# A scan and feed-forward kernel on one core: unit 0's scan in four tiles, the first transfers in halves over two queues, and a new order of the first steps

## The chip, the cores and the metric

The kernel runs on one core of one Trainium2 chip. Its engines are TensorE (PE, with its weight loads PEld), VectorE (DVE), ScalarE (ACT), GpSimd (POOL) and SyncE (SP), which here only issues transfers. The metric is the device time of one execution in microseconds. A time is the median of several runs.

## The reference: what is computed

Two blocks follow each other. The first is a chunked scan over a sequence of 768 positions, for 4 sequences (batch) of 8 heads each, with head dimension 32 and state size 16:

```
for each chunk:
    L  = exp(cum[i] - cum[j]) for i >= j, else 0        # products of the decays a
    M  = (C B^T) * L
    y  = M x  +  (C state) * exp(cum)
    state = exp(sum(log a)) * state + sum_j (B_j x_j) * exp(cum[-1] - cum[j])
```

The second is a feed-forward block on the result, 3072 tokens of 256 values: `h = y @ w_in` (256 x 2048), `g = h * cos(h)`, `out = g @ w_out` (2048 x 256). The two weights come in as 64-bit floats, the rest as 32-bit floats.

## The kernel before, in words

**Tiling.** The sequence is cut into six chunks of 128 positions. Chunk 0 is cut once more into two units of 64 positions (unit 0 and unit 1), so that TensorE gets its first large products early. A unit's partitions hold two halves s of 64 rows (sequences 2s and 2s+1), and p (or q in the loads) picks one of the two sequences of a half.

**Steps of a unit.** `spread_a` (L330) spreads the decays over the partitions with small matmuls; `decays0` (L345) turns them into products of decays with a scan on VectorE (`lam`, L353). `turn0` (L363) transposes B and C on TensorE (L370) and ScalarE copies them out of PSUM (`cut` L377, `take` L373). `reach0` (L380) is one matmul (L383) and one scan (L385) for unit 1's decays from its start. `inner` (L394) makes g = C B^T (L401), `weights` (L405) multiplies g by `lam` on VectorE (L410), and `finish0` (L413) makes y: for unit 1 first what the old state adds (L426), then M x (L434) and the new state's sum (L444); ScalarE copies y out (L454 for unit 0, L452 for unit 1) and `take_s0`, `take_s1` copy the new state (L462). `add_s1` adds the decayed old state to unit 1's on GpSimd (L469, L471). PSUM is handed out in turn: `pair` (tag "scan", two buffers of two banks), tags "h" and "o" (two buffers of one bank each). A new tile of a tag waits until the tile two before it has been read.

**Weights.** `fetch` (L195) loads a piece of w_in or w_out, 512 KB each, eight of either. A piece is turned from 64-bit to 32-bit words in two steps: `grade` (L213) is two activations on ScalarE (L227, L225) and one operation on GpSimd (L228); `join` (L235) is two operations on VectorE (L241, L243) and one on GpSimd (L251), which writes the finished piece. For the first piece `grade` and `join` go by halves (n=2).

**Feed-forward steps.** A step n covers 256 tokens' worth of one unit and 256 of the 2048 columns. `first(n)` is the product with w_in (L649), `wind(n)` the range reduction (ScalarE L654, VectorE L656), `gate(n)` the sine (ScalarE L661), `gated(n)` the product h * cos(h) (VectorE L666), `second(n)` the product with w_out (L710). In chunk 0 the steps alternate between unit 0 (even n) and unit 1 (odd n); steps 2j and 2j+1 need piece j of w_in and of w_out. `hp`, the result of `first`, has two buffers, so `first(n)` waits for `gated(n-2)`.

**Order.** The whole order is written out by hand: within an engine, instructions run in the order in which the program issues them. `first_steps` (L892) holds the steps 0 to 3 of the feed-forward block together with the rest of unit 1's scan; from step 4 on a loop (L948) takes over, in which a step does `first`, `wind`, `grade` of the next piece, `gate`, `join` of this step's piece, `gated`, the scans of chunk 1 (`halved`, L877, VectorE L496), and `second(n-2)`. In the opening transfers go through the queue of SP, save the two pairs of loads of C for units 0 and 1, which are issued from ScalarE's queue (L125); a transfer's issue stands in the order of its engine like any other instruction. `clips` (L835) prepares the decays for later chunks and writes them to memory, after which chunk 1's loads start. `fill` (L81) issues matmuls whose result nobody reads.

The two places in the order that the prediction comes back to, the opening and the first steps, are these lines of the kernel before:

```
    spread_a(0, 0, (0, 1), wide[0])
    spread_a(0, 1, (0,), wide[1])
    cut0, take0 = turn0(0, [bank([P, 2, P], "tp", "h") for _ in range(2)])
    spread_a(0, 1, (1,), wide[1])
    spread_a(1, 0)
    for p in range(2):
        decays0(0, p)
```

Of the kernel before, what the change touches and what calls it, by code (L numbers as in the profile page):

```python
# [25 lines left out]
def kernel(  # L26
# [91 lines left out]
    def load_bc(k, which=(0, 1), eng=nc.sync):  # L118

        if k not in bcs:  # L120
            both = loads.tile([P, 2, 2, 2, H, N], FP32, tag="bc", name="bc")
            bcs.update({i: both[:, i] for i in range(2)})
        for w in which:
            for s in range(2):
                eng.dma_start(out=bcs[k][s * W:(s + 1) * W, w].rearrange("p q h n -> p (q h) n"),  # L125
                              in_=(B, C)[w][2 * s:2 * s + 2, :, k * W:(k + 1) * W, :]
                              .rearrange("b h i n -> i (b h) n"))

    def load_x(k):
# [3 lines left out]
        for s in range(2):  # L133
            nc.sync.dma_start(out=xrs[k][s * W:(s + 1) * W].rearrange("p q h d -> p (q h) d"),
                              in_=x[2 * s:2 * s + 2, :, k * W:(k + 1) * W, :]
                              .rearrange("b h i d -> i (b h) d"))
# [98 lines left out]
    def join(which, i, es=(0, 1)):  # L235


        parts = held.get((which, i), ())
        for e in es[:len(parts)]:
            high, bits, last = parts[e]  # L240
# [12 lines left out]
    load_bc(0, (0,))  # L253
    load_bc(0, (1,), nc.scalar)
    fetch("in", 0)
    load_x(0)
    load_bc(1, (0,))
    fetch("in", 1)
    load_x(1)
# [12 lines left out]
    load_bc(1, (1,), nc.scalar)  # L272
# [33 lines left out]
    share_a(1, G, 0, H)  # L306
    G.memset(along1[:, :, 0:1], 0.0)
    G.tensor_scalar(out=a0[:, 1], in0=a0[:, 1], **clip)
    for p in range(2):
# [9 lines left out]
                    axis=mybir.AxisListType.XY, op=ALU.add)  # L319

# [9 lines left out]
    def spread_a(k, p, parts=(0,), tile_=None):  # L330

        n = 2 if tile_ else 1
        if (k, p) not in spread:
            spread[k, p] = [t.rearrange("p (h i) -> p h i", i=W) for t in (
                [tile_[:, i, 0:H * W // 2] for i in range(2)] if tile_ else
                [bank([P, H * W], "a_ps", "o")])]
        for i in parts:
            for s in range(2):
                b = 2 * s + p
                PE.matmul(spread[k, p][i][s * W:(s + 1) * W],  # L340
                          lhsT=those[:, b:b + 1].to_broadcast([P, W]),
# [3 lines left out]
    def decays0(k, p):  # L345

        if p == 0:
            lams[k] = scan.tile([P, 2, H, W], FP32, tag="lam", bufs=4, name="lam")
# [682 lines left out]
```

## Time and profile before

| what | value |
|---|---|
| three runs | 377.05, 378.02, 380.63 us; median 378.02 us |
| the profiled execution | 377.81 us, of which the span of the profile is 376.0 us |
| granted TensorE clock | 0.998 of full speed |
| busy share: PE, PEld | 97 %, 87 % |
| busy share: DVE, POOL, ACT | 75 %, 57 %, 46 % |
| moved by transfers | 31.54 MB in 124425 packets, 93568 of them under 512 B |

The profile is of one execution. Its times are microseconds from the start of the span. A group is a line of the program on one engine with its operation and its tile; behind a group or an instruction stands the idle time of its engine just before it and what ended that idle time. The chain of waits follows the work that ended last back from the end. A window is a stretch of the span with the busy time of each engine in it. Matmuls overlap each other in TensorE, so a busy PE is not one at its peak.

### The profile page before, as it was taken

Reading aid. Unit: us, or ns where it says so; the run is one execution under the profiler, and the core shown is the slowest. Engines: PE = TensorE matmul, PEld = TensorE weight load, DVE = VectorE, ACT = ScalarE, POOL = GpSimd, SP = SyncE. Lnnn points to the kernel's source line nnn. Section 1 sums busy time; section 2 is a strip of 40 time slices with the busy share of each in tenths; the row PEclk is TensorE's granted clock in tenths of the full one; section 3 lists DMA queues with packets and bytes.
Section 4 is the critical chain, followed back from the end, with each engine's and each line's share of the span. In section 5 each row is a group of like instructions: output and inputs, shape, how many; then the busy total and the mean of one; then the engine's idle time right before and its main releaser. Section 6 shows DMA issues by size and latency. Waiting matters only on the chain.

```text
span 376.0 us, 8691 instructions
## 1 busy us (share of the span) xinstructions
PE 365.3 (97%) x3274; PEld 326.0 (87%) x3274; DVE 281.7 (75%) x471; ACT 172.7 (46%) x295; POOL 215.1 (57%) x336
## 2 busy tenths in 40 slices
PE   8978999999999999999999999999999999999995
PEld 4667887888899899999899998999999989999994
DVE  5958999989889957987767987766887872553553
ACT  3586576444354335344434445434444443444442
POOL 5568664489947545674454693363775344544451
PEclk9999999999999999999999999999999999999999
DMA  9999987415536641745223654211020000010011
GB/s 123 227 272 249 254 210 143 98 14 132 127 84 81 125 109 16 125 114 136 28 42 33 124 140 94 51 16 16 3 40 8 13 17 2 2 28 2 5 26 28
DMA packets 124425, 31.54 MB, mean 84 GB/s; under 512 B 93568, under 2 KB 120288, under 8 KB 124384
## 3 DMA queue, kind: packets, MB, share of 16 engines
q1 hardware_dynamic: 120064, 30.60, 38.3%
q10 hardware_dynamic: 4320, 0.39, 0.9%
q8 instruction: 26, 0.43, 0.5%
q14 instruction: 15, 0.12, 0.1%
HBM read 27.64 MB, written 3.34 MB: 82 GB/s over the span
## 4 chain that ended last, share of the span: by engine, by line
PE 71%; POOL 7%; DVE 7%; SPq 5%; DMA 5%; issue 3%; ACT 1%; POOLq 0%; DVEq 0%; ACTq 0%
PE hp L649 34%; PE o L748 30%; SPq L151 3%; POOL words L685 2%; PE y L588 2%; DMA xr<-in_x_dram 2%; PE g L546 2%; DVE mag L243 1%; DVE mag L241 1%; DMA words<-in_moe_w_out_dram 1%; PE y L581 1%; DVE w L656 1%; POOL gd L691 1%; DVE gT L666 1%; SPq L110 1%
## 5 line engine op out<-in xcount | busy, mean ns | idle before, releaser
L649 PE MATMUL hp<-yT,w_in 128*128 128x256 f32 x768 | 183.4, 382 | 3.8 <-POOL la L838 1.9
L649 PEld LDWEIGHTS hp<-yT,w_in 128*128 128x128 f32 x768 | 139.4, 190 | 23.5 <-issue 5.9
L691 POOL TENSOR_TENSOR gd<-gT 128x256 f32<-128x256 f32 x79 | 59.0, 747 | 99.5 <-DVE gT L666 93.0
L661 ACT ACTIVATE w<-w,quarter 128x512 f32<-128x512 f32 x96 | 69.2, 721 | 78.8 <-DVE w L656 78.8
L656 DVE SCALAR_TENSOR_TENSOR w<-hp,k 128x512 f32<-128x512 f32 x96 | 65.4, 681 | 39.5 <-ACT k L654 39.1
L654 ACT ACTIVATE k<-hp 128x512 int32<-128x512 f32 x96 | 57.1, 595 | 81.2 <-PE hp L649 80.9
L666 DVE TENSOR_TENSOR gT<-hp,w 128x512 f32<-128x512 f32 x96 | 65.2, 680 | 34.5 <-ACT w L661 25.7
L748 PE MATMUL o<-words,gd 128*128 128x128 f32 x474 | 65.9, 275 | 0.0
L748 PEld LDWEIGHTS o<-words,gd 128*128 128x128 f32 x474 | 59.3, 192 | 0.0
L496 DVE TENSOR_TENSOR_SCAN lam<-arow,unit 128x512 f32<-128x512 f32 x40 | 56.8, 1421 | 0.0
L748 PEld LDWEIGHTS o<-w_out,gT 128*128 128x128 f32 x316 | 47.5, 191 | 4.0
L748 PE MATMUL o<-w_out,gT 128*128 128x128 f32 x316 | 48.0, 274 | 0.0
L694 POOL TENSOR_TENSOR gd<-gT,gd 128x128 f32<-128x128 f32 x79 | 44.4, 562 | 6.2
L693 POOL TENSOR_TENSOR gd<-gT,gd 128x128 f32<-128x128 f32 x79 | 44.0, 556 | 6.2
L710 PE MATMUL o<-w_out,gT 128*128 128x256 f32 x128 | 30.2, 380 | 1.2 <-POOL w_out L251 1.2
L567 DVE TENSOR_TENSOR m<-g,lam 128x256 f32<-128x256 f32 x80 | 30.9, 415 | 0.5
L748 PE MATMUL o<-words,gT 128*128 128x128 f32 x158 | 30.6, 275 | 0.0
L748 PE MATMUL o<-w_out,gd 128*128 128x128 f32 x158 | 30.5, 275 | 0.0
L710 PEld LDWEIGHTS o<-w_out,gT 128*128 128x128 f32 x128 | 24.2, 190 | 4.8 <-POOL w_out L251 1.6
L748 PEld LDWEIGHTS o<-words,gT 128*128 128x128 f32 x158 | 24.0, 192 | 0.0
L748 PEld LDWEIGHTS o<-w_out,gd 128*128 128x128 f32 x158 | 24.0, 192 | 0.0
L765 DVE TENSOR_TENSOR sum<-ps,sum 128x256 f32<-128x256 f32 (+1 forms) x27 | 16.7, 645 | 0.6
(104 smaller groups left out, 268.2 us busy)
## 6 DMA issues: line engine op xcount, KB each, us to landing
arow<-a_cut SPq DMA_DIRECT2D x20, 512.0 KB
words<-in_moe_w_in_dram SPq DMA_DIRECT2D x8, 512.0 KB
words<-in_moe_w_out_dram SPq DMA_DIRECT2D x8, 512.0 KB
out_dram<-sum SPq DMA_DIRECT2D x18, 128.0 KB
blocks<-in_B_dram SPq DMA_DIRECT2D x128, 8.0 KB
blocks<-in_C_dram SPq DMA_DIRECT2D x128, 8.0 KB
xr<-in_x_dram SPq DMA_DIRECT2D x14, 128.0 KB
along<-a_all SPq DMA_DIRECT2D x20, 64.0 KB
```

Of the source, the lines that this page charges most:

```text
L496: V.tensor_tensor_scan(out=lam[c, b][:, hs].rearrange("p h i -> p (h i)"), data0=rows_.rearrange("p h i -> p (h i)"), data1=unit[:, b % 2 ...
L567: V.tensor_tensor(out=m_[js, :, :, is_], in0=g_[js, :, :, is_], in1=l_[js, :, :, is_], op=ALU.mult)
L649: PE.matmul(to_[:, e], lhsT=w_in[:, k, fs], rhs=y[:, k], start=(k == 0), stop=(k == KT - 1), skip_group_check=True)
L654: ACT.activation(k, hp[n], AF.Copy, bias=0.25, scale=INV_2PI)
L656: V.scalar_tensor_tensor(out=w, in0=hp[n], scalar=INV_2PI, in1=k, op0=ALU.mult, op1=ALU.subtract)
L661: ACT.activation(cos, cos, AF.Sin, bias=quarter, scale=TWO_PI)
L666: V.tensor_tensor(out=gT[n], in0=hp.pop(n), in1=cos, op=ALU.mult)
L691: G.tensor_tensor(out=d[:, 0:2], in0=g[:, 1:2].to_broadcast([P, 2, P]), in1=g[:, 3::-3], op=ALU.subtract)
L693: G.tensor_tensor(out=d[:, 2], in0=g[:, 0], in1=d[:, 0], op=ALU.subtract)
L694: G.tensor_tensor(out=d[:, 3], in0=g[:, 2], in1=d[:, 2], op=ALU.subtract)
L710: PE.matmul(o[c, u][:, t], lhsT=g[:, 2 * e + t], rhs=w_out[:, 2 * j + e], start=(j == e == t == 0), stop=(j == NJ - 1 and e == 1), skip_gr ...
L748: PE.matmul(at[q], lhsT=a_[q], rhs=w[q], start=(j == 0 and q in starts), stop=(j == NJ - 1), skip_group_check=True)
```

## The change

**Transfers of chunk 0.** `load_bc` and `load_x` now issue one half (s) at a time and take the queue to issue on. x of unit 0 and of unit 1, and B and C of unit 1, are split: one half goes through SP's queue, the other through ScalarE's. Two of ScalarE's four issues behind the first pair stand where C of unit 1 was issued before; the other two stand later, one behind `take0(0)` (half of B of unit 1) and one behind `grade("in", 0)` (half of x of unit 1).

**Unit 0's scan.** The four quarters of its decays go to four PSUM tiles, where before two tiles held two quarters each; the scans are issued as the quarters come. The decays of unit 1 are shared out on VectorE (`share_a(1, V, 0, H)`), where GpSimd did it before.

**Order of the opening.** The scan of `reach0` comes ahead of unit 0's g; `spread_a(1, 0)` comes behind unit 0's g, and `spread_a(1, 1)` behind unit 1's transposes, which are issued as part of the opening now. The first weight piece is graded and joined whole.

**Order of the first steps.** Unit 1's g (`inner`, now one call for each half t) is issued between the two halves of `first(0)`. The `fill` ahead of unit 1's `weights` goes. `grade("in", 1)` and `units_of_decay` come ahead of unit 1's `weights`. The grading of a piece is moved by one place against the joins; `second(0)` and `second(1)` stand ahead of and behind `first(3)`, where both came behind it; `take_s1` comes one step later, and `add_s1` moves from step 2 to step 6 in the loop.

```diff
-    def load_bc(k, which=(0, 1), eng=nc.sync):
+    def load_bc(k, w, s, eng=nc.sync):
...
             bcs.update({i: both[:, i] for i in range(2)})
-        for w in which:
-            for s in range(2):
-                eng.dma_start(out=bcs[k][s * W:(s + 1) * W, w].rearrange("p q h n -> p (q h) n"),
-                              in_=(B, C)[w][2 * s:2 * s + 2, :, k * W:(k + 1) * W, :]
-                              .rearrange("b h i n -> i (b h) n"))
-    def load_x(k):
+        eng.dma_start(out=bcs[k][s * W:(s + 1) * W, w].rearrange("p q h n -> p (q h) n"),
+                      in_=(B, C)[w][2 * s:2 * s + 2, :, k * W:(k + 1) * W, :]
+                      .rearrange("b h i n -> i (b h) n"))
+    def load_x(k, s, eng=nc.sync):
         if k not in xrs:
...
             xrs.update({i: both[:, i] for i in range(2)})
-        for s in range(2):
-            nc.sync.dma_start(out=xrs[k][s * W:(s + 1) * W].rearrange("p q h d -> p (q h) d"),
-                              in_=x[2 * s:2 * s + 2, :, k * W:(k + 1) * W, :]
-                              .rearrange("b h i d -> i (b h) d"))
+        eng.dma_start(out=xrs[k][s * W:(s + 1) * W].rearrange("p q h d -> p (q h) d"),
+                      in_=x[2 * s:2 * s + 2, :, k * W:(k + 1) * W, :]
+                      .rearrange("b h i d -> i (b h) d"))
...
-    def join(which, i, es=(0, 1)):
-        parts = held.get((which, i), ())
-        for e in es[:len(parts)]:
-            high, bits, last = parts[e]
+    def join(which, i):
+        parts = held.pop((which, i), ())
+        for e, (high, bits, last) in enumerate(parts):
             V.tensor_scalar(out=bits, in0=bits, scalar1=3, scalar2=0x3FFFFFFF,
...
-    load_bc(0, (0,))
-    load_bc(0, (1,), nc.scalar)
+    for s in range(2):
+        load_bc(0, 0, s)
+        load_bc(0, 1, s, nc.scalar)
     fetch("in", 0)
-    load_x(0)
-    load_bc(1, (0,))
+    load_x(0, 0)
+    load_bc(1, 1, 1)
+    load_bc(1, 0, 0)
     fetch("in", 1)
-    load_x(1)
+    load_x(1, 0)
     fetch("out", 0)
...
     ACT.activation(const.tile([P, 1], FP32, name="sine"), quarter, AF.Sin)
-    load_bc(1, (1,), nc.scalar)
+    load_x(0, 1, nc.scalar)
+    load_bc(1, 1, 0, nc.scalar)
     V.memset(a0z[:, :, 0:1], 0.0)
...
     share_a(0, V, 0, 6)
-    share_a(1, G, 0, H)
     G.memset(along1[:, :, 0:1], 0.0)
...
                     axis=mybir.AxisListType.XY, op=ALU.add)
+    share_a(1, V, 0, H)
...
-    def spread_a(k, p, parts=(0,), tile_=None):
-        n = 2 if tile_ else 1
-        if (k, p) not in spread:
-            spread[k, p] = [t.rearrange("p (h i) -> p h i", i=W) for t in (
-                [tile_[:, i, 0:H * W // 2] for i in range(2)] if tile_ else
-                [bank([P, H * W], "a_ps", "o")])]
-        for i in parts:
-            for s in range(2):
-                b = 2 * s + p
-                PE.matmul(spread[k, p][i][s * W:(s + 1) * W],
-                          lhsT=those[:, b:b + 1].to_broadcast([P, W]),
-                          rhs=a0s[k][:, i * H // n:(i + 1) * H // n], start=True, stop=True,
-                          tile_position=(0, s * W), skip_group_check=True)
-    def decays0(k, p):
-        if p == 0:
+    def spread_a(k, p, i=0, n=1, tag="o"):
+        ps = (pair("a_ps")[:, 0] if tag is None else bank([P, 4 * P], "a_ps", tag))
+        ps = spread[k, p, i] = ps[:, 0:H * W // n].rearrange("p (h i) -> p h i", i=W)
+        for s in range(2):
+            b = 2 * s + p
+            PE.matmul(ps[s * W:(s + 1) * W], lhsT=those[:, b:b + 1].to_broadcast([P, W]),
+                      rhs=a0s[k][:, i * H // n:(i + 1) * H // n], start=True, stop=True,
+                      tile_position=(0, s * W), skip_group_check=True)
+    def decays0(k, p, i=0, n=1):
+        if p == i == 0:
             lams[k] = scan.tile([P, 2, H, W], FP32, tag="lam", bufs=4, name="lam")
         flat = "p h i -> p (h i)"
-        parts = spread.pop((k, p))
-        for i, ps in enumerate(parts):
-            hs = slice(i * H // len(parts), (i + 1) * H // len(parts))
-            V.tensor_tensor_scan(out=lams[k][:, p, hs].rearrange(flat), data0=ps.rearrange(flat),
-                                 data1=unit0[:, hs].rearrange(flat), initial=0.0,
-                                 op0=ALU.mult, op1=ALU.add)
+        hs = slice(i * H // n, (i + 1) * H // n)
+        V.tensor_tensor_scan(out=lams[k][:, p, hs].rearrange(flat),
+                             data0=spread.pop((k, p, i)).rearrange(flat),
+                             data1=unit0[:, hs].rearrange(flat), initial=0.0,
+                             op0=ALU.mult, op1=ALU.add)
...
-    def inner(k):
-        gs[k] = g = [pair("g") for _ in range(2)]
+    def inner(k, t):
+        gs[k, t] = g = pair("g")
         bT, cT = turns0[k][:, 0], cuts[k]
-        for p, s, q in ((p, s, 2 * t + q) for t in range(2) for p in range(2) for s in range(2)
-                        for q in range(2)):
-            ss, r = slice(s * W, (s + 1) * W), slice(32 * q, 32 * q + 32)
-            PE.matmul(g[q // 2][ss, q % 2, p * P:(p + 1) * P].rearrange("p (t i) -> p t i", t=2),
+        for p, s, q in ((p, s, q) for p in range(2) for s in range(2) for q in range(2)):
+            ss, q_ = slice(s * W, (s + 1) * W), 2 * t + q
+            r = slice(32 * q_, 32 * q_ + 32)
+            PE.matmul(g[ss, q, p * P:(p + 1) * P].rearrange("p (t i) -> p t i", t=2),
                       lhsT=bT[r, p, ss], rhs=cT[r, p, :, ss], start=True, stop=True,
-                      tile_position=(32 * q, s * W), skip_group_check=True)
+                      tile_position=(32 * q_, s * W), skip_group_check=True)
...
                 for ap in (units[k], lams[k]))
-        V.tensor_tensor(out=m, in0=gs[k][q][:, :, 0:2 * P].rearrange("p k (s i) -> p k s i", s=2),
+        V.tensor_tensor(out=m, in0=gs[k, q][:, :, 0:2 * P].rearrange("p k (s i) -> p k s i", s=2),
                         in1=l, op=ALU.mult)
...
-    def first(n):
+    def first(n, between=None):
         c, f = divmod(n, NF)
...
                           start=(k == 0), stop=(k == KT - 1), skip_group_check=True)
+            if between and e == 0:
+                between()
...
     fill(bank([P, 2, P], "warm", "o"), 1)
-    wide = [pair("a_ps") for _ in range(2)]
-    spread_a(0, 0, (0, 1), wide[0])
-    spread_a(0, 1, (0,), wide[1])
-    cut0, take0 = turn0(0, [bank([P, 2, P], "tp", "h") for _ in range(2)])
-    spread_a(0, 1, (1,), wide[1])
-    spread_a(1, 0)
-    for p in range(2):
-        decays0(0, p)
+    spread_a(0, 0, 0, 2, None)
+    spread_a(0, 0, 1, 2, None)
+    spread_a(0, 1, 0, 2, "h")
+    for p, i in ((0, 0), (0, 1), (1, 0)):
+        decays0(0, p, i, 2)
+    cut0, take0 = turn0(0, [bank([P, 2, P], "tp", "o") for _ in range(2)])
+    spread_a(0, 1, 1, 2, "h")
+    decays0(0, 1, 1, 2)
     cut0()
     take0(0)
+    load_bc(1, 0, 1, nc.scalar)
     scan_reach = reach0(1)
+    scan_reach()
     weigh0(0)
-    grade("in", 0, n=2)
-    inner(0)
-    spread_a(1, 1)
-    scan_reach()
+    grade("in", 0)
+    load_x(1, 1, nc.scalar)
+    for t in range(2):
+        inner(0, t)
+    spread_a(1, 0)
     for q in range(2):
...
     take_s0, _ = finish0(0)
+    cut1, take1 = turn0(1, [pair("tp")[:, 0].rearrange("p (k i) -> p k i", k=4)])
+    spread_a(1, 1)
     for p in range(2):
...
+    def both(k):
+        for t in range(2):
+            inner(k, t)
     def first_steps():
...
-        cut1, take1 = turn0(1, [pair("tp")[:, 0].rearrange("p (k i) -> p k i", k=4)])
         cut1()
...
         take1(1)
-        first(0)
-        inner(1)
+        first(0, lambda: both(1))
         weigh_c(1)
         weigh0(1)
-        fill(bank([P, 4, P], "warm", "o"), 1)
+        rest = grade("in", 1, later=True)
+        rest()
+        units_of_decay()
         for q in range(2):
             weights(1, q)
-        rest = grade("in", 1, later=True)
         wind(0)
-        rest()
-        units_of_decay()
+        rest = grade("out", 0, later=True)
         take_s1, add_s1 = finish0(1)
...
         gate(0)
-        rest = grade("out", 0, later=True)
+        rest()
+        clips()
         gated(0)
-        rest()
         wind(1)
-        take_s1()
-        clips()
+        join("out", 0)
         first(2)
...
         gate(1)
-        join("out", 0)
+        take_s1()
         rest()
         gated(1)
+        second(0)
         wind(2)
+        join("in", 2)
         first(3)
...
         gate(2)
-        join("in", 2)
         rest()
         gated(2)
-        add_s1()
+        second(1)
         wind(3)
-        second(0)
+        join("out", 1)
         rest = grade("in", 3, later=True)
         gate(3)
-        join("out", 1)
         rest()
         gated(3)
-        second(1)
         rest = grade("out", 2, later=True)
...
         rest()
-    first_steps()
+        return add_s1
+    add_s1 = first_steps()
     rest_of_loads()
...
             gated(n)
+            if n == AHEAD + 2:
+                add_s1()
             for do in (*behind, *unsummed):
...
             unsummed.clear()
```

## Prediction

> **What bounds the kernel now.** I read the page's slices first (TensorE is busy nearly throughout, the clock full), then stretches of the span, to see where TensorE still waits:
>
> ```profile
> core 0: us, PE busy (x) PEld busy (x) DVE busy (x) ACT busy (x) POOL busy (x), PEclk, DMA share, GB/s
> ...
> 13.33:21.56 8.23, 7.77 (x178) 5.65 (x179) 5.40 (x8) 5.81 (x14) 4.79 (x8) 1.00 1.10 298
> 21.56:35.25 13.69, 10.63 (x50) 9.04 (x49) 10.41 (x16) 10.09 (x18) 10.63 (x15) 1.00 0.90 262
> 35.25:60.70 25.45, 25.08 (x117) 21.31 (x115) 25.02 (x33) 16.61 (x29) 16.32 (x17) 1.00 0.87 212
> ```
>
> From 35.25, where first(5) starts, TensorE is idle for 0.37 of 25.45 us; its sums there are fixed work that the change leaves alone. What can be won is the time at which that work starts. But in the same row VectorE is busy for 25.02 of 25.45: an earlier TensorE is worth only what VectorE is earlier too. In 13.33 to 35.25 TensorE stands still for 0.46 (y copied out), 1.88, 1.18, and 1.13 of "busy" is the fill. So some 4.6 us are the most that order can win there.
>
> Then the chain of waits, for the opening:
>
> ```profile
> 4.22 7.11 DMA xr<-in_x_dram
> ...
> 11.38 0.72 PE y L434 x45
> 12.11 0.47 PE y L444 x23
> 12.60 0.59 ACT yT L454
> ...
> 13.33 1.97 PE hp L649 x8
> ```
>
> The second half of unit 0's x lands at 11.34, and y, its copy and first(0) follow. The timeline shows what is just behind it:
>
> ```profile
> 5.93 1.27 DVE L353 TENSOR_TENSOR_SCAN lam<-a_ps,unit 128x256 f32<-128x256 f32 x2 [2.41 <-PE a_ps L340]
> 7.70 1.27 DVE L353 TENSOR_TENSOR_SCAN lam<-a_ps,unit 128x256 f32<-128x256 f32 x2 [0.50 <-PE a_ps L340]
> 9.87 1.26 DVE L410 TENSOR_TENSOR m<-g,lam 128x512 f32<-128x512 f32 x2
> 12.47 0.42 PEld L370 LDWEIGHTS tp<-ident,bc 128*128 128x128 f32 x4
> 15.20 0.68 POOL L391 TENSOR_TENSOR rT<-turned,m 128x256 f32<-128x256 f32 x1 [1.45 <-DVE lam L353]
> 15.95 1.29 DVE L410 TENSOR_TENSOR m<-g,lam 128x512 f32<-128x512 f32 x2 [0.82 <-PE g L401]
> 23.44 3.61 PE L649 MATMUL hp<-yT,w_in 128*128 128x256 f32 x16 [1.88 <-POOL la L838]
> 24.42 1.26 POOL L251 TENSOR_TENSOR w_out<-mag,last 128x512 uint32<-128x512 uint32 x1
> 32.17 1.48 DVE L241 TENSOR_SCALAR mag<-mag 128x512 uint32<-128x512 uint32 x1 [1.08 <-POOL mag L228]
> 33.41 1.99 PE L710 MATMUL o<-w_out,gT 128*128 128x256 f32 x8 [1.18 <-POOL w_out L251]
> 35.18 1.12 DVE L241 TENSOR_SCALAR mag<-mag 128x512 uint32<-128x512 uint32 x1
> ```
>
> Unit 0's `weights` end at 11.13, only 0.21 before x. Unit 1's transposes at 12.47 wait for the last half of its B: the trace has it landed at 12.56. The 1.88 ahead of first(2) is put down to `clips` on POOL, which it does not need; first(2)'s weight load had run at 21.25 and w_in's piece was done at 20.32. The trace has packets of 16384 bytes on the queue "q8 instruction" at 14.12, 20.89 (1.07 long) and 25.93, and TensorE stops at its 705th recorded instruction: I read this as TensorE waiting for its program.
>
> **Scan in four tiles.** Now the first scan waits for all four products into its tile (5.93). With a tile per quarter it starts 0.13 behind its own: those end at 5.04, so 5.17. By 7.70 three scans are done, one 0.69 scan is left instead of two (1.27): 0.6 earlier. The product of `reach0` no longer stands behind spread_a(1, 0) (1.03 of TensorE), so it runs at 7.5, g at 8.1 to 8.9, the reach scan (0.70) at 8.33, and `weights` (1.26) at 8.98 to 10.24: 0.9 earlier. The moved share_a(1) (384 wide took 0.56 on VectorE, so 512 wide some 0.75) fits the 2.41 idle ahead of 5.93; without that cover it would cost 0.75.
>
> **Small transfers.** Half of x takes the queue position of half of C, so x lands by 9.8 (the first half's 9.69 plus 0.1) instead of 11.34. What is late next is `weights`: y takes 1.17 from 11.38 to 12.55, so now 10.24 to 11.45, copied by 12.05. But the transfers up to unit 1's B are the same bytes, and with both queues in use the small ones land one after the other now (4.21, 4.96, 5.66, 6.53, 7.60, by turns from ACT and SP). So B is complete at 12.56 as before, the transposes end at 13.13 as before, and TensorE runs in order: spread_a(1, 1), moved behind them, takes 1.08 to 14.15. first(0) starts at 14.0, not 13.33: a loss of 0.7. SP's queue issues one small transfer less ahead of w_in's piece 1 and two less ahead of w_out's piece 0 (0.6 to 0.8 each); the pieces still land one behind the other, 1.1 to 1.8 apart, until 26.5, so this is worth nothing. The Trainium skill's page "DMA: Bandwidth & Descriptors" (Rules for kernel authors) speaks against this part: transfers to two partition halves serialize, and more issuing queues save only issue time. By that rule the halves are worth nothing; by the rows x still gains 1.5 from its place in the order, and the sum is the same, since B holds it.
>
> **First piece whole.** Now its halves are done at 12.60 and 13.75. After: ACT from 8.71 (0.7), POOL 0.61, then on VectorE behind `weights` 0.42 and 0.69, POOL 1.27: 12.7. Ahead of 14.0, so it costs nothing; if ACT starts later than 10.0 it costs.
>
> **Unit 1's g and y.** g waits for take_s0 (14.86) and take1(1) (15.12) on ACT, which hang on the transposes and stay. Now it runs behind first(0), 15.22 to 16.02; then at 14.9 and 15.3 to 15.65, between its halves. `lam` of unit 1 is late next: scan behind spread_a(1, 1), 14.2 to 15.4 (now ended 15.13). `weights` then 15.45 to 16.75 instead of 15.95 to 17.24: 0.5 earlier. The fill goes for nothing, since y waits for `weights`. y ends 1.87 later, 18.6 (19.11). first(0)'s second half ends at 16.4 and its range reduction at 17.7, ahead of the join of w_in's piece 1, so that is as now (20.3). first(1) starts at 19.05, ends at 20.9.
>
> **Program refill.** A packet holds some 250 instructions (0.43 MB for 6548 matmuls and weight loads), and the 705th is again the start of first(2). I take its refill to be asked for one packet earlier, in unit 1's y; that comes 0.5 earlier, so first(2) starts at 22.9. Bounds: 20.9 (refilled in time) and 23.44. The page "Runtime: NRT & Kernel Launch" (Instruction fetch mechanics) calls refills of 256 instructions mostly hidden; by that first(2) would start at 20.9. No term of the sum hangs on it, because of what comes next.
>
> **Order of the steps.** first(1) at 20.9 leads through ACT (0.60) and VectorE (0.69) to `join("out", 0)`: 22.35 to 23.5, POOL 1.27 to 24.8 (now 25.68; its mag no longer stands ahead). second(0) 24.85, first(3) 26.6, second(1) 28.3, first(4) 30.1 (1.73 each), second(2) 31.8. But POOL's next mag (0.61) now stands behind each L251 (1.27), so a join is 3.1 behind the one before it: `join("out", 1)` is done at 32.3, so second(2) at 32.3 and first(5) at 34.05: TensorE leads by 1.2. `clips` runs from 20.3 on POOL instead of 21.75, so its two writes and chunk 1's loads behind them on SP's queue (which waited 4.1 for it) go out 1.4 earlier, behind the pieces: nothing. `take_s1` feeds only add_s1, so its later place is free.
>
> **add_s1** (2.2 on POOL at 29.36) goes from there to step 6. VectorE's 1.08 wait at 32.17 stays (mag at 32.9), so w of step 4 is only 0.3 earlier (34.58 now). L241 and L243 behind it took 1.12 and 0.98 beside POOL, 0.41 and 0.69 alone; POOL has less beside them, so I take half, 0.5: VectorE leads by 0.8 from step 5, and by 0.3 at least. At step 6 add_s1 falls beside a busy VectorE: at worst one L241 goes from 0.41 to 0.84; I take 0.2. POOL itself has room there (16.32 of 25.45 busy). **Sum**: 0.8 - 0.2 = 0.6 us. Against the profiled execution (377.81: the span and 1.8 around it) that is 377.2; the median of the runs is 0.2 above it.
>
> **Rivals.** *All of TensorE's lead comes through*: 1.2, and VectorE's waits that stop first(9), first(12) and chunk 1's y (0.21, 0.23, 0.34) go too: 375.8. For it: VectorE's long rows are contention that may move. Against: 25.02 of 25.45.
> *Nothing comes through*: VectorE leads by 0.3, add_s1 takes 0.4: 377.9.
> *Slower: ScalarE stands at an issue.* ScalarE's fourth issue sat from 3.1 to 4.22, until the first transfer of its queue had landed (4.21), so an issue can wait for a transfer. Behind the new issue after take0 stand L227 and L225 of the first piece, behind the second one the copy of y (L454) and unit 1's transposes. Bounds: no wait (ACT is idle for 0.96 there, an issue takes 0.63 to 0.82), or a wait for w_in's piece 1 (14.27), which puts B of unit 1 some 4.8 later. The nearest row is the last transfer of ScalarE's own queue, 10.45: issue 0.7, landing 3.3 behind it, so B at 14.45 instead of 12.56: 1.9 against the gain of 0.6, 379.1. It decides when B lands later than 13.2.
> *The halves don't do what they say* is in the sum: worth nothing already.
>
> **How the numbers follow.** Chances: forecast 0.42 (376.7 to 377.7 by its own bounds), all of it 0.20, nothing 0.18, slower 0.20. The range reaches from the first rival less 0.4 to the slower one plus 0.3: 375.4 to 379.4. A change under 1% can hardly be told from none here, since the three runs lie 0.9% apart. Faster by over 1% (below 374.2) would need most of the 4.6: 0.07. Slower by over 1% (above 381.8) needs the far end of the last rival: 0.09. Within: 0.84.
>
> **What would show it.** Four scans of L353 from 5.2, `weights` done near 10.2, no wait of y for x; transposes still near 12.5, first(0) near 14.0; y of unit 1 ending near 18.6; the gap ahead of first(2) still there; second(0) at 24.9; first(5) near 34.1; VectorE busy as now in 35 to 60. Wrong if the transposes move, if an issue on ScalarE waits past 9.3, or if VectorE's lead at step 5 is not 0.3 to 1.2.

## The result, and the profile after

The changed kernel takes 391.48 us (median of 4 runs, 390.11 to 391.81), the kernel before 378.75 us beside it (377.05 to 380.63): a ratio of 1.0328, interval 1.0269 to 1.0387. I had forecast 377.2 us in a range of 375.4 to 379.4. The profiled execution took 390.11 us with a span of 388.3 us, 12.3 more than before.

The stretches of the span that the prediction started from, in the changed kernel (columns: stretch, its length, then busy time and number of instructions of each engine, granted clock, share of the DMA engines, GB/s):

```profile
core 0: us, PE busy (x) PEld busy (x) DVE busy (x) ACT busy (x) POOL busy (x), PEclk, DMA share, GB/s
13.33:21.56 8.23, 1.43 (x4) 0.58 (x6) 1.29 (x2) 0.64 (x2) 1.26 (x1) 0.58 1.12 304
21.56:35.25 13.69, 11.03 (x189) 7.39 (x186) 8.01 (x12) 9.32 (x21) 7.20 (x12) 0.87 0.39 91
35.25:60.70 25.45, 24.51 (x104) 20.33 (x103) 19.70 (x28) 14.84 (x26) 16.11 (x17) 0.94 0.91 242
```

The first row says it: TensorE is busy for 1.43 of 8.23 us, where it had 7.77 before, and its clock falls to 0.58. Yet the DMA engines are as busy as before (1.12). VectorE, which the prediction made the limit of the last row (25.02 of 25.45), has room there now: 19.70.

The chain of waits in the opening and the first steps (start, length, what):

```profile
0.75 3.28 DMA bc<-in_C_dram
4.05 6.19 DMA bc<-in_C_dram
10.26 9.83 DMA bc<-in_B_dram
20.82 1.91 PE a_ps L335 x4
22.73 2.01 PE hp L642 x4
29.07 2.01 PE hp L642 x8
34.96 3.68 PE o L705 x8
```

Before, the second half of unit 0's x and then y stood here. Now it is one transfer of 64 KB: half of unit 1's B, issued at 10.26 on ScalarE, which had waited for its own half of C (landed at 10.24). It takes 9.83 us. Behind it stand products at nearly twice their length: 1.98 for a spread that takes 1.08 at full clock, 3.68 for a `second` that takes 1.99.

The timeline around them (start, length, engine, line, operation, tiles; in brackets the idle time before and what ended it). Unit 0's scan is L345, weights L403, transposes L363, spread L335, `first` L642, `second` L705, `clips` L836, `join` L237:

```profile
4.89 1.85 DVE L345 TENSOR_TENSOR_SCAN lam<-a_ps,unit 128x256 f32<-128x256 f32 x3 [0.80 <-PE a_ps L335]
7.43 0.69 DVE L345 TENSOR_TENSOR_SCAN lam<-a_ps,unit 128x256 f32<-128x256 f32 x1 [0.68 <-PE a_ps L335]
8.74 1.26 DVE L403 TENSOR_TENSOR m<-g,lam 128x512 f32<-128x512 f32 x2
10.26 0.62 ACTq L123 DMA_DIRECT2D bc<-in_B_dram  x1
20.13 0.69 PE L363 MATMUL tp<-ident,bc 128*128 128x128 f32 x2 [8.55 <-DMA bc<-in_B_dram]
20.75 1.98 PE L335 MATMUL a_ps<-m,those 128*64 128x512 f32 x4
22.65 2.08 PE L642 MATMUL hp<-yT,w_in 128*128 128x256 f32 x4
25.46 1.29 DVE L403 TENSOR_TENSOR m<-g,lam 128x512 f32<-128x512 f32 x2 [1.46 <-PE g L394]
29.07 3.72 PE L642 MATMUL hp<-yT,w_in 128*128 128x256 f32 x16 [0.46 <-ACT yT L445]
30.66 0.40 POOL L836 TENSOR_SCALAR cut<-a_in 96x256 f32<-96x256 f32 x1
34.96 3.68 PE L705 MATMUL o<-w_out,gT 128*128 128x256 f32 x8 [2.17 <-POOL w_out L247]
```

Up to unit 0's y all went as forecast: scans from 4.89, weights done at 10.00, both halves of unit 0's x landed (7.76 and 9.59) before they are wanted, y without a wait. Then TensorE stands still for 8.55 us. The granted clock is full until 14.60, half until 24.84, full until 35.08, half until 38.49, and full from there to the last few us. From step 12 on every step is 12.4 to 12.5 us behind the kernel before, to the end.

The start of some steps in the profiled executions, for all kernels of this document (us):

| kernel | first(0) | first(1) | first(3) | first(7) | first(12) |
|---|---|---|---|---|---|
| before | 13.33 | 19.57 | 25.17 | 42.15 | 60.76 |
| changed | 22.66 | 29.07 | 38.46 | 53.90 | 73.22 |
| e1: half of B back on SP | 13.78 | 23.72 | 32.93 | 48.36 | 67.67 |
| e2: before, half of B late | 16.26 | 23.96 | 29.14 | 45.53 | 64.14 |
| e3: half of B early on ScalarE | 13.99 | 27.17 | 36.68 | 52.11 | 71.43 |
| e4: halves of B and x on SP | 13.74 | 19.62 | 27.33 | 42.77 | 62.08 |
| e5: x on SP, half of B late | 19.22 | 26.04 | 34.99 | 50.88 | 70.18 |
| e6: as e1, x in long rows | 14.55 | 19.96 | 27.67 | 43.11 | 62.43 |
| e7: as e4, old order of steps | 13.87 | 19.27 | 26.58 | 43.58 | 62.17 |
| e8: as e4, add_s1 back | 13.64 | 19.05 | 28.29 | 43.88 | 62.49 |
| e9: changed, wait filled | 21.58 | 28.85 | 36.57 | 52.00 | 71.33 |
| e10: as e4, two steps exchanged | 14.00 | 19.41 | 27.13 | 41.94 | 61.25 |
| e11: as e10, add_s1 at step 12 | 13.87 | 20.13 | 27.85 | 42.65 | 61.24 |

### The profile page after: what moved, and what is told of

It is laid out like the page before. It is cut to its first block, busy times and chain, and to the rows that moved or that the text cites. A ratio compares the mean times of both kernels' runs of the same rounds, so it can differ in the third digit from the quotient of the medians.

```text
span 388.3 us, 8681 instructions
## 1 busy us (share of the span) xinstructions
PE 368.6 (95%) x3272; PEld 326.7 (84%) x3272; DVE 281.3 (72%) x470; ACT 172.4 (44%) x293; POOL 214.6 (55%) x333
## 4 chain that ended last, share of the span: by engine, by line
PE 76%; DVE 8%; DMA 6%; POOL 5%; issue 2%; SPq 1%; ACT 1%; POOLq 0%; ACTq 0%
PE hp L642 37%; PE o L743 29%; DMA bc<-in_B_dram 3%; PE y L581 3%; DMA bc<-in_C_dram 2%; PE o L705 2%; DVE mag L239 2%; PE g L539 2%; DVE mag L237 2%; POOL words L680 2%; DVE lam L489 2%; DVE w L651 1%; PE y L574 1%; DVE gT L661 1%; POOL gd L686 1%
## 5 line engine op out<-in xcount | busy, mean ns | idle before, releaser
L642 PE MATMUL hp<-yT,w_in 128*128 128x256 f32 x768 | 184.8, 384 | 2.6 <-DVE gT L661 1.9
L642 PEld LDWEIGHTS hp<-yT,w_in 128*128 128x128 f32 x768 | 139.9, 191 | 24.7 <-issue 7.0
L661 DVE TENSOR_TENSOR gT<-hp,w 128x512 f32<-128x512 f32 x96 | 65.2, 679 | 33.7 <-ACT w L656 24.8
L743 PEld LDWEIGHTS o<-w_out,gT 128*128 128x128 f32 x316 | 47.6, 191 | 3.9
L705 PE MATMUL o<-w_out,gT 128*128 128x256 f32 x128 | 32.1, 396 | 2.7 <-POOL w_out L247 2.7
L705 PEld LDWEIGHTS o<-w_out,gT 128*128 128x128 f32 x128 | 25.1, 198 | 7.0 <-POOL w_out L247 3.5
L247 POOL TENSOR_TENSOR w_out<-mag,last 128x512 uint32<-128x512 uint32 x8 | 10.2, 1272 | 14.5 <-DVE mag L239 14.5
```

The source lines that it names most:

```text
L642: PE.matmul(to_[:, e], lhsT=w_in[:, k, fs], rhs=y[:, k], start=(k == 0), stop=(k == KT - 1), skip_group_check=True)
L661: V.tensor_tensor(out=gT[n], in0=hp.pop(n), in1=cos, op=ALU.mult)
L705: PE.matmul(o[c, u][:, t], lhsT=g[:, 2 * e + t], rhs=w_out[:, 2 * j + e], start=(j == e == t == 0), stop=(j == NJ - 1 and e == 1), skip_gr ...
L743: PE.matmul(at[q], lhsT=a_[q], rhs=w[q], start=(j == 0 and q in starts), stop=(j == NJ - 1), skip_group_check=True)
```

## The experiments

The first theory after the result was that this one transfer costs all of it. The rival was that the new order of the steps costs it.

### e1: the half of B on SP again

```diff
     load_bc(1, 0, 0)
+    load_bc(1, 0, 1)
     fetch("in", 1)
...
     take0(0)
-    load_bc(1, 0, 1, nc.scalar)
```

> The changed kernel, with one line moved: the second half of unit 1's B is issued from SP, right behind the first half and ahead of w_in's piece 1, and no longer from ScalarE behind unit 0's take. Theory (this one transfer's place costs the 12.4 us): that B is whole by 12.6 to 13.2, as before (in the changed kernel 20.09); the transposes end near 13.5, first(0) starts at 13.6 to 14.2 (22.66), no half clock in the opening, and the time is 376.5 to 379, a ratio of 0.995 to 1.003 against the kernel before. Rival (the new order of the steps and add_s1's later place cost it): B lands early all the same, but first(7) is still some 9 us or more behind the kernel before, and the ratio stays above 1.02.

Measured: 384.81 us (6 runs) against 378.09 (23 runs of the kernel before, shared by e1 to e4), ratio 1.0183 (1.0150 to 1.0216). B is whole at 12.29 and first(0) starts at 13.78, as the theory had it; the time is not. What TensorE waits for between 5 and 47 us (in total, times, longest):

```profile
PE y L428 <- DMA xr<-in_x_dram: 3.9, 1, 3.9
PE o L706 <- POOL w_out L247: 2.7, 2, 2.2
```

The second half of unit 1's x, which the change also moved to ScalarE, was issued at 11.01 and landed at 21.66 (14 of the 16 shares into which a transfer is split by 17.87, the last two at 21.46 and 21.66). The theory was half right: a transfer's place, but there are two such transfers, and the second one stands ready behind the first.

### e3: the half of B on ScalarE, but early

```diff
     load_bc(1, 1, 0, nc.scalar)
+    load_bc(1, 0, 1, nc.scalar)
...
     take0(0)
-    load_bc(1, 0, 1, nc.scalar)
```

> The changed kernel, with the same transfer still on ScalarE's queue, but issued with its other early ones, ahead of unit 0's take. If the place in time behind the pieces that SP has queued is what makes it slow, it is issued by 7, lands by 13, and the time is 376.5 to 379.5 (ScalarE may stand at the issue, ahead of the take: up to 1.5 us). If ScalarE's queue is what makes it slow, it lands 8 us or more behind its issue again, and the time is above 385.

Measured: 388.40 us (4 runs), ratio 1.0266 (1.0231 to 1.0301): the landing is that of the first case, the time that of the second, for another reason. The half of B is issued at 4.82 and landed at 11.87, so ScalarE's queue is not slow in itself. But again x is late, issued at 11.89 and landed at 25.11:

```profile
PE y L428 <- DMA xr<-in_x_dram: 7.1, 1, 7.1
PE o L706 <- POOL w_out L247: 1.6, 2, 1.1
```

### e4: the half of x on SP too

```diff
     load_x(1, 0)
+    load_x(1, 1)
     fetch("out", 0)
...
-    load_x(1, 1, nc.scalar)
```

This comes on top of e1.

> As the run with the half of B on SP, and the second half of unit 1's x is issued from SP too, behind its first half, so that ScalarE issues nothing behind unit 0's take. If ScalarE's hold at its own issues costs only through that half of B, the time is that of the other run within 0.5 us. If the hold at the issue of x still costs (the first piece's shares and the copies of y stand behind it), this one is 0.5 to 2 us faster.

Measured: 378.85 us (12 runs), ratio 1.0021 (1.0000 to 1.0042). That is 6.0 us less than e1, where at most 2 were expected: what e1 still waited for was the landing of x, and not ScalarE's hold at its issue. With both transfers on SP the loss is gone but for some 0.8 us. x of unit 1 lands at 17.29, first(1) starts at 19.62 (before: 19.57). So the two late transfers make the whole of the +3.3 % but 0.2.

### e2 and e5: the half of B late alone

e2 is the kernel before with only the half of B moved to ScalarE, behind unit 0's take. e5 is the changed kernel with x on SP, so that the half of B is late alone there too. The edit of e2 (`load_bc` also takes the halves that it issues):

```diff
     load_x(0)
-    load_bc(1, (0,))
+    load_bc(1, (0,), ss=(0,))
...
     take0(0)
+    load_bc(1, (0,), nc.scalar, (1,))
```

> The kernel before, with only this moved: the second half of unit 1's B is issued from ScalarE behind unit 0's take instead of from SP. Theory: ScalarE's sequencer stands at it until about 10.3, it lands near 20, TensorE stands still from about 12 and gets half a clock behind it, and the time is some 12 us (10 to 14) above the kernel before, 388 to 392. Rival (the new order of the steps is what costs): less than 4 us.

Measured: 380.77 us (10 runs), ratio 1.0060 (1.0038 to 1.0082). The expected 12 us did not come. Same place behind the take, issued at 10.15, but landed at 15.72: 5.6 us behind its issue in place of 9.8, and TensorE waits 2.44.

What differed was what SP had queued. In e2 both halves of x of unit 1 are in SP's queue beside it: rows of 128 bytes. In the changed kernel SP had pieces of the weights there too: rows of 2048 bytes. That gave the second theory, by packets, and e5 to try it:

```diff
     load_x(1, 0)
+    load_x(1, 1)
...
-    load_x(1, 1, nc.scalar)
```

> The changed kernel, with the second half of unit 1's x issued from SP behind its first half; the half of B stays on ScalarE behind unit 0's take. The runs so far have the half of B late alone (kernel before: 2.0 us by its span of 379.4 against 376.0, landing 15.72) and the half of x late alone (landing 21.66, ratio 1.018). Theory (the DMA engines take the packets of the two queues by turns, one for one, so that a small transfer's 64 rows per engine wait for 64 packets of the other queue: short beside rows of x, some 6.4 us beside pieces of 2048 bytes): the half of B now meets x's 128-byte rows on SP's queue and lands at 15 to 17, and the time is 379 to 384. If a late half of B costs by itself what the changed kernel showed (landing 20.09), it is 387 or more.

Measured: 387.18 us (4 runs, against 378.23, 29 runs shared by e5 to e8), ratio 1.0229 (1.0200 to 1.0257). The landing lies where the second theory put it: issued at 9.70, 15 of its 16 shares landed by 15.31, the last at 16.59 (changed kernel: 16.52 and 20.09). Whether the theory's reason put it there is taken up behind e6. The time does not follow: 379 to 384 was expected and it is 387. Only 4.9 us of it are the wait:

```profile
PE tp L364 <- DMA bc<-in_B_dram: 4.9, 1, 4.9
PE o L706 <- POOL w_out L247: 2.7, 2, 2.2
```

The granted clock is half from 15.42 to 22.24 and from 32.48 to 35.90. The spread that the change put behind these transposes takes 1.97 and the first half of first(0) 2.08 us, 1.8 more than at full clock, and the first `second` 3.27 in place of 1.99. e2 has half clock too (15.93 to 19.34), at first(0), but waits 2.4 us less. So in the changed order a late B costs its wait and then some 3 us more (first(12) is 8.1 behind e4's); in e2 first(12) is 3.4 behind the kernel before, 0.9 more than the wait.

### e6: the same bytes in long rows

The packets of the two queues in the changed kernel, from 16.6 to 23.1, while the half of x moves (queue, number of packets, MB, share of the 16 DMA engines). q10 has packets only while a transfer that ScalarE issued is under way; q1 carries SP's:

```profile
q1 hardware_dynamic: 1080, 2.06, 96.2%
q10 hardware_dynamic: 1058, 0.13, 15.2%
```

The two queues move the same number of packets, 1080 and 1058, though one moves 2.06 MB and the other 0.13. In e5, while the half of B moves (12.8 to 14.8), q1's are rows of x, and both go fast:

```profile
q1 hardware_dynamic: 1266, 0.24, 108.0%
q10 hardware_dynamic: 926, 0.06, 34.5%
```

So the engines seem to take a packet of each queue by turns. A small transfer of 1024 rows then has 64 packets per engine. Beside pieces of the weights, each of them waits for one packet of q1, which takes 93 ns (0.962 x 16 x 6.5 / 1080), and takes 15 itself (0.152 x 16 x 6.5 / 1058): 64 x 0.108 = 6.9 us. That is an estimate from the very stretch that it explains, so it tests nothing by itself. e6 puts it to the test: the late half of x, at the same place on the same queue and of the same 128 KB, but in 64 rows (they are other elements of x, so unit 1's y is not the reference's).

```diff
-    load_x(1, 1, nc.scalar)
+    nc.scalar.dma_start(out=xrs[1][W:2 * W].rearrange("p q h d -> p (q h d)"),
+                        in_=x[2].rearrange("h (p e) d -> h p (e d)", e=H * 2)
+                        .rearrange("h p n -> (h p) n")[0:W])
```

This is on top of e1.

> As the run with the half of B back on SP, so that only the second half of unit 1's x is late on ScalarE's queue (there it landed at 21.66, 10.65 behind its issue, time 384.8). Here the same 128 KB are read at the same place in 64 rows of 2048 bytes in place of 1024 rows of 128: other elements of x, so y of unit 1 is computed from wrong data. Theory (packets by turns, one for one): four packets per engine in place of 64, so it lands within 1.5 us of the time at which the queue reaches it, by 17.5, and the time falls to that with x on SP, 378 to 380. Rival (ScalarE's queue comes after SP's whatever the packets, or the bytes share the bandwidth): it lands at 20 or later and the time stays at 383 to 386.

Measured: 380.02 us (10 runs), ratio 1.0055 (1.0031 to 1.0079). Issued at 11.71, 15 of 16 shares landed by 16.32, the last at 17.72; TensorE's wait of 3.9 for unit 1's x is gone. Of the 6.0 us between e1 (384.81) and e4 (378.85), 4.8 are back by the size of the rows alone. From 13.5 to 16.5 ScalarE's queue moves its 0.13 MB in 78 packets, where 0.13 MB were 1058 above:

```profile
q1 hardware_dynamic: 1051, 0.65, 79.7%
q10 hardware_dynamic: 78, 0.13, 22.9%
```

The Trainium skill's page "DMA: Bandwidth & Descriptors" (Queues, rings and completion order) says that each engine goes round the queues it has work for by packets; the equal counts above and e6 agree with it, and it is the rule to which the prediction had paid no heed.

For the half of B it explains less than the theory had it. These are the changed kernel's packets from 10.9, where the issue of that half ended, to 14.5 (the first line), and from 14.5 to 15.5:

```profile
q1 hardware_dynamic: 1463, 0.98, 101.7%
q1 hardware_dynamic: 225, 0.15, 70.8%
q10 hardware_dynamic: 975, 0.06, 68.7%
```

Up to 14.5 q10 has no packet: what SP had issued before this transfer (the rest of w_in's piece 1, half of x, nearly all of w_out's piece 0) moved first. Then nearly the whole half of B moved within 1 us. Only its last share, at 20.09, met the later pieces of the weights. In e5 it was issued ahead of w_out's piece 0 (9.70 against 10.68), and its first row moved at 12.41. So its place in the order of issue over both queues goes with its late start, and turns by packets with its last share only; no run tells the two apart for B, and why it started so late was not tried. In e1, too, it is only the last two shares of x that moved beside the weights (q10 has 102 packets from 17.5 to 21.5).

### e7 and e8: what the rest of the change is worth

e7 is e4 with the steps behind first(0) in the order of the kernel before, add_s1 too, without the fill: the new opening alone. e8 is e4 with add_s1 alone put back.

```diff
         second(1)
+        add_s1()
         wind(3)
...
-            if n == AHEAD + 2:
-                add_s1()
```

> The new opening alone, with both late halves on SP: scan in four tiles, x of unit 0 in halves over two queues, g of unit 1 between the halves of first(0), no fill; behind first(0) the steps are in the order of the kernel before, with add_s1 in its old place. Theory (in the run with the new order VectorE reached step 5 0.63 us late, 35.21 against 34.58 for its second w, since join of w_in's piece 3 stood behind POOL's): here that w is at 34.3 to 34.7, first(11) within 0.4 of the kernel before, and the time 376.5 to 378.5, ratio 0.996 to 1.001. Rival (the opening itself costs): not faster than the run with the new order, 378.9.

> The new opening with both late halves on SP and the new order of steps, but add_s1 back ahead of wind(3) in the opening's steps. Theory (add_s1's later place cost 0.5 to 0.7: in the run with it first(11) and first(12) went from 0.59 to 1.31 behind the kernel before): first(12) is 0.5 to 0.9 behind in place of 1.31, and the time is 378 to 378.6. Rival (2.2 us more of POOL ahead of join of w_in's piece 3 is worse, since VectorE already waits 1.44 for POOL there): first(7) 1.2 to 2.5 behind in place of 0.62, time 379.3 to 381.

Measured: e7 378.29 us (12 runs), ratio 0.9997 (0.9979 to 1.0016); e8 379.09 (12 runs), 1.0015 (0.9993 to 1.0036). The new opening is worth nothing by itself, as its first steps show: first(0) 0.54 later, first(1) 0.30 earlier. What was expected of e7 behind them did not come: in its profiled execution (379.27) TensorE stood still for 3.49 within first(2), the range reduction that started at 34.58 in the kernel before starts at 36.00, and first(11) is 1.4 behind the kernel before. e8 can't be read: its profiled execution had half clock from 25.21 to 28.62, where e4 had none, so that it fits the rival's number (first(7) 1.73 behind) for another reason. The intervals of e4, e7 and e8 overlap.

### e9: TensorE kept busy during the wait

```diff
+    fill(bank([P, 4, P], "warm", "o"), 7)
     cut1, take1 = turn0(1, [pair("tp")[:, 0].rearrange("p (k i) -> p k i", k=4)])
```

This is the changed kernel, with both late halves.

> The changed kernel with both late halves, and seven fills of TensorE (1.1 us each, products that nothing reads) behind unit 0's y, where TensorE waits 8.55 us for the half of B. Nothing else moves. Theory (part of the 12.4 us is the granted clock, 0.5 from 14.60 to 24.84 behind that wait: spread 1.98 in place of 1.08, first half of first(0) 2.08 in place of 1.13): the transposes still start at 20.1, first(0) at 21.6 to 21.9 in place of 22.66, first(1) at 27.0 to 27.6 in place of 29.07 or, if x of unit 1 holds it there, at 28.0; with 1.85 more if the second half-clock stretch (35.08 to 38.49) goes too. Time 386.5 to 390.5. Rival (the lower clock costs nothing that x's late landing doesn't cost anyway): first(1) within 0.3 of 29.07 and the time at 391.

Measured: 392.49 us (4 runs, 388.27 to 393.37; against 378.35, 23 runs shared by e9 to e11), ratio 1.0338 (1.0286 to 1.0390): above the expected 386.5 to 390.5, and not faster than the changed kernel (1.0328). Its profiled execution is the one of 388.27. There the clock is full throughout the steps, and the two parts come out as follows. first(0) starts 1.08 earlier (21.58), but first(1) only 0.22 (28.85), since the half of x then holds y: the rival's answer. The second stretch of half clock is gone, and first(3) is 1.89 earlier (36.57), which stays to the end. The wait for w_out's piece is still there:

```profile
PE o L705 <- POOL w_out L247: 2.7, 2, 2.2
PE tp L363 <- DMA bc<-in_B_dram: 2.5, 1, 2.5
PE y L427 <- DMA xr<-in_x_dram: 0.5, 1, 0.5
```

The other three executions took 391.82 to 393.37 at a mean clock of 0.986 to 0.990 (profiled: 0.998), so they had half clock somewhere in spite of the fills. What the clock costs is thus shown for one execution only, and that a fill buys it back is not shown.

### e10 and e11: the rest of the loss

In e4 VectorE is late at step 5, as this stretch of its timeline shows. The join of w_in's piece 3 waits for its mag on GpSimd, and the second range reduction behind it (`wind`, L653) starts at 35.21; in the kernel before it started at 34.58:

```profile
33.74 0.82 DVE L237 TENSOR_SCALAR mag<-mag 128x512 uint32<-128x512 uint32 x1 [1.44 <-POOL mag L225]
34.60 0.69 DVE L239 SCALAR_TENSOR_TENSOR mag<-words,mag 128x512 uint32<-128x512 uint32 x1
35.21 0.68 DVE L653 SCALAR_TENSOR_TENSOR w<-hp,k 128x512 f32<-128x512 f32 x1
```

e10 exchanges two steps of e4, and e11 moves add_s1 to step 12 as well:

```diff
+        rest = grade("in", 3, later=True)
         join("out", 1)
-        rest = grade("in", 3, later=True)
...
-            if n == AHEAD + 2:
+            if n == NF - 4:
                 add_s1()
```

> The new opening and order with both late halves on SP, and two steps exchanged: w_in's piece 3 is graded ahead of the join of w_out's piece 1, so that its mag on POOL runs before that join's POOL operation and not behind it. Theory (VectorE reached step 5 0.63 later than in the kernel before because this mag came 1.44 late): the wait of 1.44 ahead of that join goes, the second w behind it starts at 33.7 to 34.2 in place of 35.21, first(7) is 0 to 0.8 ahead of the kernel before in place of 0.62 behind, and the time is 377 to 378. Rival (TensorE's own gaps hold it): within 0.3 of 378.9.

> As the run with the two steps exchanged, and add_s1 at step 12 instead of step 6. Theory (at step 6 its 2.6 us of POOL lie beside VectorE's joins and lengthen them: first(11) and first(12) lost 0.46 and 0.24 there): these 0.7 go, and the time is 0.3 to 0.7 below the other run. Rival (at step 12 VectorE is just as full, or the state comes too late for chunk 1's y): no gain, or up to 1.5 us worse.

Measured: e10 378.84 us (12 runs), ratio 1.0010 (0.9989 to 1.0031); e11 377.98 (12 runs), 1.0000 (0.9972 to 1.0027). In e10's profile the wait of 1.44 is gone:

```profile
32.30 1.12 DVE L237 TENSOR_SCALAR mag<-mag 128x512 uint32<-128x512 uint32 x1
33.46 0.98 DVE L239 SCALAR_TENSOR_TENSOR mag<-words,mag 128x512 uint32<-128x512 uint32 x1
34.36 0.68 DVE L653 SCALAR_TENSOR_TENSOR w<-hp,k 128x512 f32<-128x512 f32 x1
```

But the two operations of the join, now beside GpSimd's, take 1.12 and 0.98 in place of 0.82 and 0.69, so 0.85 of the 1.44 is left (35.21 to 34.36). first(7) goes from 0.62 behind the kernel before to 0.21 ahead; first(12) is 0.49 behind, for add_s1 at step 6. In e11 first(7) and first(12) stand 0.50 and 0.48 behind, no loss between them, so step 12 is the better place. That profiled execution started its first(1) 0.72 later than e10's, and its time was the longest of its 12 (382.66). e10's time is the rival's (within 0.3 of 378.9). By the times, no version beats the kernel before by what can be measured; the best of them, e11, equals it.

## Why the prediction was wrong, step by step

**The step that failed** stands under "Small transfers": "the transfers up to unit 1's B are the same bytes, ... So B is complete at 12.56 as before". The bytes are the same, but one half of B no longer stood among them. It was issued at 10.26, behind the take, and SP had by then queued w_in's piece 1 (8.07), half of x (9.16) and w_out's piece 0 (9.80), which it had had to issue behind that half of B before. No row of the half moved until 14.5, when these were nearly through, and B was whole at 20.09. All three of the prediction's own signs of being wrong came: the transposes moved (20.13), an issue on ScalarE waited past 9.3 (10.26), and VectorE had no lead of 0.3 at step 5, not even with the transfers put back (e4). For the half of x I worked out nothing at all, though it stood even later and e1 shows that it costs 1.8 % with B in time.

**The slower rival** had the right mechanism at its start and the wrong size behind. ScalarE's sequencer stood at the issue until 10.26 (I took 10.45) and the issue took 0.62 (0.7). The landing, 3.3 us behind the issue, was the mis-sized term: it measured 9.2 behind the end of the issue. Landings of that size are those of the kernel before, small transfers beside other rows of 64 and 128 bytes (the last half of its B: 3.1 behind the end of its issue). The far end of the rival moved only the wait and kept that 3.3, so the range missed it too. Its sum was also off: an issue from 14.27 on, by the rival's own 0.7 and 3.3, puts B 5.7 later, not 4.8. Nor was lateness worth its own length: I priced B's 1.9 us as 1.9. Comparing the changed kernel with e4, which differs by the two transfers alone, the last transposes are done and the spread behind them starts 8.0 later (20.75 against 12.73), the spread takes 0.9 more and first(0)'s first half 0.95, e4 loses 0.5 at first(1) that the changed kernel does not, and the first `second` takes 1.7 more: 11.1, which is the distance of their first(12) (73.22 against 62.08). (The changed kernel also waits 1.9 longer ahead of that `second`, but e4 loses the same 1.9 within first(2).) Of this, 3.5 is half clock.

**Why the two losses don't add up.** By the ratios, B late alone (e5) is +2.3 %, x late alone +1.8 % (e1) or +2.7 % (e3), both +3.3 %. Both are waits for transfers under way at the same time: in the changed kernel x landed at 26.00, before y asked for it (27.41).

**Scan in four tiles**: right. Weights done at 10.00 (forecast 10.24), x at 9.59 (9.8), y without a wait. It is worth nothing, as forecast, because B comes next: e4 starts first(0) at 13.74 (14.0) and ends unit 1's y at 18.68 (18.6). With the change's transfers it is worth nothing either.

**First piece whole**: the condition that I named came true. ScalarE began it at 10.93, later than 10.0, since it stood at the issue; the piece was done at 14.90 (12.7). It hid behind B. In e4 it was done at 13.27; first(0)'s weight load waited 0.81 for it, but TensorE was at the spread until 13.81.

**Program refill**: the gap ahead of first(2) is not there in the changed kernel. In e4 it comes within first(2), behind its fourth product and 1.63 long, and first(2) ends at 25.23; the forecast start of 22.9 plus some 1.9 gives 24.8.

**Order of the steps**: TensorE's forecast lead was there, with the transfers in place, but smaller: e4's first(5) at 35.02 (before 35.25, forecast 34.05). The prediction's 32.3 for `join("out", 1)` does not follow from the 3.1 a join beside it, which from 24.8 gives 31.0; in e4 these joins were done at 25.45, 29.06 and 33.12, 3.6 and 4.1 apart. VectorE's lead of 0.8 was a lag of 0.63. I had kept its wait for the mag of w_in's piece 3 and put that mag at 32.9; it ran from 33.09 to 33.7, behind the join's own operation on GpSimd (31.84 to 33.12). And the 0.5 that I took off the next join's two operations did not come: they took 1.12 and 0.98, as before. e10 shows that the order of these two steps was the larger part: VectorE is 0.85 earlier with them exchanged.

**add_s1**: 0.2 was too little. From first(10) to first(12) e4 loses 0.7 against the kernel before (0.59 to 1.32 behind), and with add_s1 at step 12 nothing is lost there.

**The sum** of these steps without the transfers, -0.6, is +0.8 by the medians of e4 (ratio 1.0021, lower end 1.0000).

## What to carry to other kernels

When a small transfer is moved to another queue, look up what the first queue has been given by the time of its issue: the half of B moved no row until that was nearly through (10.88 to 14.5). Then count rows, not bytes: beside rows of 2048 bytes the half of x, 64 rows per engine, took some 7 us, and the same bytes in 64 rows in all did not (e6). Short-rowed transfers that are wanted early go on the queue ahead of the long-rowed ones, or early enough that they meet only their like; an issue that stands behind other work of a busy sequencer is neither. Price a late operand at its wait plus what TensorE loses to its clock behind it, here 3.5 us behind a wait of 8.6, in e2 at most 1 behind 2.4.

## What the runs showed that was not expected

One of the 16 shares of a transfer falls behind in most of these profiles, above all behind the first 16384-byte packet of the queue named "q8 instruction" (at 13.55 in the changed kernel, 1.40 long; at 12.96 in e1, 13.62 in e3). In the pieces of the weights it is late by 1.2 to 2.1 us in the changed kernel, e1 and e3, by some 0.1 in e8. Up to then, in the changed kernel, the last of a transfer's 16 shares lands within 0.1 us of the one before it, but for a half of unit 0's x (0.8); from then on 1.6 to 2.0 later. For the half of B that made 3.57: 15 shares had landed by 16.52, the last at 20.09. The last 64 of its 1024 rows, one engine's worth, moved after 16.0, beside rows of 2048 bytes. That the packet causes the lag was not tried, and it is not all of it: in e2 one share was 0.5 to 0.7 behind from 7.0 on, and the first such packet came at 15.54.

The granted clock fell to half 3.0 us into the wait (11.58 to 14.60) and came back at 24.84, 4.7 us after TensorE had work again. The Trainium skill's page "TensorE: Matmul & The Clock Gate" (What's actually happening) puts both the fall and the return at some 3.4 us of idle or busy time; the fall came a little sooner here and the return took longer, in e3 7.9 us (25.16 to 33.04). And waits of 2.17 ahead of the same `second` went with half clock in the changed kernel (35.08 to 38.49) and without it in e9's profiled execution.
